# Order and PSUM banks of the last two down products in a nine-block attention + SwiGLU kernel

## The chip, the cores and the metric

The kernel runs on one NeuronCore of one Trainium2 chip. The metric is the device time of one execution in microseconds (us); the time before is the median of three executions. A profile is a separate, traced execution of the same kernel.

## What is computed

The reference, cut to what matters:

```python
# q, k, v: (8 batches, 8 heads, 576 positions, 64) ; g_norm: (64)
kv  = einsum('bhsd,bhse->bhde', k, v)
att = einsum('bhsd,bhde->bhse', q, kv)
x   = att / sqrt(mean(att * att, axis=-1) + 1e-6) * g_norm   # then laid out as (4608 tokens, 512)
g   = x @ w_gate                                             # 512 -> 1536
h   = g * (1 / (1 + exp(-g))) * (x @ w_val)                  # 512 -> 1536
out = h @ w_out                                              # 1536 -> 512, all float32
```

Only the last line, `out = h @ w_out` (called "down" in the code), is touched by the change, and only for the last 1024 of the 4608 tokens.

## The kernel before, in words

The 4608 tokens are cut into nine blocks of 512 (`BLK`), numbered 0 to 8 (`NB` = 9). For each block, attention makes `x`, the "up" step makes `h` (1536 features on partitions, 512 tokens), and the "down" step makes 512 rows of the output. Blocks 0 to 2 go one at a time (`alone`); blocks 3 to 8 go in pairs (3,4), (5,6), (7,8) (`Pair`). In a pair, up is done for both blocks together and then down for the first block (`pair.a.down`) and for the second (`pair.b.down`). After the pair (7,8) no block is left, so the last two downs are called with `nxt` = None and no attention work lies between their matmuls. The code's own loop order, together with `in_order` for TensorE, fixes the order of the matmuls there; the other engines run their instructions in the order in which the program issues them, each when its semaphores allow.

**Down as seven products.** `Down` (line 977, on top of `Quad`, line 640) multiplies a 2x2 arrangement of quarter matrices in the Winograd form of Strassen's method: seven products P1 to P7 instead of eight. Each product has 12 matmuls (two tiles e of 128 tokens, six steps over the features), each shown by the profile as 2 rows, so 24 rows. The results are put together like this, where o1 is the upper 256 tokens, o2 the lower 256, and left and right are the 256-column halves of the output:

```
S  = P1              o1 left  = S  + P2
U2 = P1 + P6         o1 right = U2 + P5 + P3
U3 = U2 + P7         o2 right = U3 + P5
                     o2 left  = U3 + P4
```

**Which bank a product goes to** is said by `CHAIN` (line 629). P1, P6, P7 and P4 are accumulated one onto another in one bank called b; P5 and P3 in a bank c; P2 has bank a. PSUM has eight banks here: b has 3 buffers, c has 2, a has 1, and a pool m has 2, which the last two downs leave unused. As U2 and U3 are partial sums inside bank b, ScalarE copies the bank out after P1 (`after1`, line 677), after P6 (`after6`, line 681), after P7 (`after7`, line 1043) and after P4 (`after4`, line 1047), and the next product of the chain can go into the bank only when the copy has read it.

For the very last block (`final`, block 8) the c bank is two banks, one for each tile e (`apart`), and P3 runs tile by tile (`order`, line 1011: all six steps of e = 0, then all six of e = 1), so that the first tile can be added and stored while the second is multiplied.

**What the operands wait for.** P7, P5 and P4 multiply sums of weight quarters that GpSimd makes (`turn_t`). P5 multiplies `s1`. P7 multiplies S3, which VectorE makes in place after P1 (`turn_s3`, line 1029), and P3 multiplies S4, which VectorE makes in place after P2, in `after2` (line 1037; in the profile these are rows of line 131, 128x1536, 1.75 us each). The S4 instruction comes after P2 because it overwrites P2's operand.

**The loop around it** is `Ffn.down` (line 1118). With `nxt` = None its order is 1, 5, 6, 7, 2, 4, 3. `after7` takes the ring buffer that o1 and o2 live in. The block's outputs are stored from `store` (line 1078) on SyncE's queue: o2 after P4 (512 KB), o1 after P3 (512 KB); in the last block o1 left after P2 (256 KB) and each tile of o1 right by itself (128 KB).

Of the kernel before, what the change touches and what calls it, by code (L numbers as in the profile page):

```python
# [8 lines left out]
F32 = mybir.dt.float32  # L9
# [5 lines left out]
P = 128  # L15
# [3 lines left out]
def kernel(  # L19
# [41 lines left out]
    nc = tc.nc  # L61

    B, H, S, D = q.shape
    NT, DM = out.shape
# [3 lines left out]
    HB = BLK // 2  # L68
    HD = DM // 2
# [10 lines left out]
    def pool(name, bufs, **kw):  # L80
        return ctx.enter_context(tc.tile_pool(name=name, bufs=bufs, **kw))
# [13 lines left out]
    m_psum = pool("m_psum", 2, space=PS)  # L95
# [34 lines left out]
    add = lambda e, o, a, b: e.tensor_tensor(out=o, in0=a, in1=b, op=OP.add)  # L130
# [21 lines left out]
    def ring():  # L152

        return r_pool.tile([P, 4, BLK], F32, name="r")

    class Words:
# [12 lines left out]
        def __init__(self, src, shape):  # L169
            self.raw = ld_pool.tile([P, LD], U32, name="ld")[:, 0 : 2 * BLK]  # L170
            dst = self.raw.rearrange("p (a b) -> p a b", a=shape[0])
            self.sent = nc.sync.dma_start(out=dst, in_=src)
            self.shape = shape
            self.begun = False
# [465 lines left out]
    class Quad:  # L640
# [11 lines left out]
        def multiply(self, p):  # L652
            name, first = CHAIN[p]
            if first:
                tiles = [PSUMS[name].tile([P, 2, HB], F32, name=name) for _ in range(1 + (name in self.apart))]
                self.ps[name], self.apart[name] = tiles[0], tiles[-1]
            banks = self.ps[name], self.apart[name]
            for e, i in self.order(p):
                lhsT, rhs = self.operands(p, e, i)

                self.ffn.multiplied = nc.tensor.matmul(  # L661
                    banks[e][:, e], lhsT=lhsT, rhs=rhs, start=first and i == 0 and (e == 0 or banks[0] is not banks[1]),
                    stop=i == self.steps - 1, skip_group_check=True,
                )
            getattr(self, f"after{p}", lambda: None)()

        def order(self, p):
            return [(e, i) for e in range(2) for i in range(self.steps)]
# [10 lines left out]
        def after6(self):  # L679
            self.u2 = self.piece(1)  # L680
            nc.scalar.copy(out=self.u2, in_=self.ps["b"])

    class Up(Quad):
# [22 lines left out]
        def after2(self):  # L706
            add(nc.vector, self.s, self.ps["a"], self.s)

        def after7(self):
            self.u3 = self.piece(2)  # L710
            copied = nc.scalar.copy(out=self.u3, in_=self.ps["b"])

            with tc.issue_after(copied.ins):
                nc.scalar.activation(out=self.s, in_=self.s, func=ACT.Silu)
            added = add(nc.vector, self.u3, self.ps["c"], self.u3)

            owed, self.ffn.owed = self.ffn.owed, None
            if owed:
                with tc.issue_after(added.ins):
                    owed()  # L720
# [232 lines left out]
    def chunks(t):  # L953

        return t.rearrange("p f (s c) -> p (f s) c", c=P) if len(t.shape) == 3 else t.rearrange("p a b c -> p (a b) c")

    def kept_steps(j, room):


        for i, (t, os) in enumerate(kept(j)):  # L960
            b11, b12, b22 = t[:, :, 0, 0], t[:, :, 0, 1], t[:, :, 1, 1]
            to = room[:, 8 * i : 8 * (i + 1)].rearrange("p (o r) c -> p o r c", r=4)
            t2_ = to[:, :, 0]
            yield lambda b22=b22, b12=b12, t2_=t2_: sub(nc.vector, t2_, b22, b12)
            yield lambda b11=b11, t2_=t2_: add(nc.vector, t2_, t2_, b11)
            yield lambda t=t, t2_=t2_, to=to: sub(
                nc.vector, to[:, :, 2:4], t[:, :, 1], t2_.unsqueeze(2).to_broadcast([P, 2, 2, P])
            )
            yield lambda t2_=t2_, os=os: send_leaf(j, os, (6,), t2_)
            yield lambda b11=b11, t2_=t2_, to=to: sub(nc.vector, to[:, :, 1], b11, t2_)  # L970
            yield lambda to=to, os=os: send_leaf(
                j, os, (7, 4, 5), to[:, :, 1:4].rearrange("p o r c -> p o (r c)")
            )
        if j < 2:
            yield from raw_steps(j)

    class Down(Quad):
        def __init__(self, ffn):
            super().__init__(NP)
            self.ffn = ffn  # L980
            self.t = {}
            self.final = ffn.n == NB - 1
            self.opens = None
            self.keeps = False
            if self.final:
                self.apart["c"] = None
# [13 lines left out]
                    )  # L1000
                self.t[p] += [t[:, 0], t[:, 1]]

        def multiply(self, p):
            super().multiply(p)
            if p in self.t and not self.keeps:
                stream.free(("T", p))
            if p == 7 and self.opens:
                stream.enable(self.opens)
            stream.pump()

        def order(self, p):
            order = [(e, i) for e in range(2) for i in range(self.steps)]
# [13 lines left out]
        def turn_s3(self):  # L1026

            pairs = self.ffn.h.rearrange("p (j e) t -> p e j t", e=2)
            sub(nc.vector, pairs[:, 0, :, 0:HB], pairs[:, 0, :, HB:BLK], pairs[:, 1, :, HB:BLK])

        def after2(self):
            add(nc.vector, self.o1[:, :, 0:HD], self.ps["a"], self.s)
            if self.final:
                self.ffn.store(self.o1[:, :, 0:HD], 0, slice(0, HD))

            pairs = self.ffn.h.rearrange("p (j e) t -> p e j t", e=2)
            self.s4 = sub(nc.vector, pairs[:, 1, :, 0:HB], pairs[:, 1, :, 0:HB], pairs[:, 0, :, HB:BLK])

        def after7(self):
            o = ring()  # L1040
            self.o1, self.o2 = o[:, 0:2], o[:, 2:4]
            u3 = self.piece(2)
            nc.scalar.copy(out=u3, in_=self.ps["b"])
            self.add_c(self.o2[:, :, HD:DM], u3)
# [21 lines left out]
    class Ffn:  # L1066
# [51 lines left out]
        def down(self, nxt, then={}):  # L1118

            down = self.down_  # L1120
            fill = nxt.steps() if nxt else {}
            for p in (1, 6, 5, 7, 2, 4, 3) if 5 in fill else (1, 5, 6, 7, 2, 4, 3):
                if p == 1 and 7 not in down.t:
                    down.turn_t(7, self.ended)
                if p == 6 and 4 not in down.t:
                    down.turn_t(4, nxt.halves[0] if nxt and nxt.n >= TURNED else None)

                with tc.issue_after(nxt.multiplied.ins) if self.n == 0 and p in (5, 6) else ExitStack():
                    down.multiply(p)
                self.make(12)  # L1130
                if p in fill:
                    fill[p]()
                if p in then:
                    then[p]()
                if p in (5, 7) and self.n == 1:

                    with tc.issue_after(nxt.scaled.ins), tc.issue_after(nxt.placed.ins):
                        for step in kept_steps(2 + (p == 7), chunks(ring() if p == 7 else xi_alone)):
                            step()
                if p == 1:  # L1140

                    with tc.issue_after(nxt.q_turned.ins) if self.n == 0 else ExitStack():
                        down.turn_s3()

        def plain_up(self, f, halves=(0, 1)):

            if 0 in halves:
                self.ps[f] = [pool.tile([P, 2, HB], F32, name=pool.name[0]) for pool in (b_psum, c_psum)]
            of = slice(halves[0], halves[-1] + 1)
            ps = [t[:, of] for t in self.ps[f]]  # L1150
            x = self.att.x[:, 0:4].rearrange("p (h m) i t -> p (m i) h t", h=2)
            for t, w in zip(ps, (wg, wv)):
                for i in range(NS):
                    nc.tensor.matmul(
                        t, lhsT=w[f // 2][:, i, P * (f % 2) : P * (f % 2 + 1)], rhs=x[:, i, of],
                        start=(i == 0), stop=(i == NS - 1),
                    )
            h = self.h[:, f].rearrange("p (h t) -> p h t", h=2)[:, of]
            nc.scalar.activation(out=h, in_=ps[0], func=ACT.Silu)
            mul(nc.vector, h, h, ps[1])  # L1160
# [208 lines left out]
    for n in range(PAIRED, NB, 2):  # L1369
        pair = Pair(n)  # L1370
        after = blocks[n + 2 : n + 5]
        fill = {}
        if after:
# [9 lines left out]
            fill = {5: first_kv, 11: second_kv}  # L1383
# [45 lines left out]
```

## Time and profile before

| | |
|---|---|
| median of three executions | 1023.85 us (1022.38 to 1024.58) |
| the profiled execution: its own time | 1026.13 us |
| the profiled execution: span of the profile | 1024.4 us |
| TensorE busy | 998.7 us, 97% of the span |
| VectorE / ScalarE / GpSimd busy | 667.3 / 232.1 / 369.8 us |
| mean granted TensorE clock | 0.997 |
| down of block 7, first matmul to the first of block 8 | 946.42 to 983.65 us |
| down of block 8, first matmul to the end of the last | 983.65 to 1021.01 us |

How to read the profile: times are counted from the start of the span. PE is TensorE's matmuls, PEld its weight loads, DVE is VectorE, ACT ScalarE, POOL GpSimd, SPq SyncE's queue, from which the stores are issued. A row of a timeline has the start, the length, the engine, the line of the kernel, the operation and "output<-input" by the names of the tiles; consecutive rows of a kind are merged with their number (x24), and what stands in brackets is how long the engine had been idle before and what the profile takes for the releaser. Matmuls overlap: a row of 24 lasts 5.34 us, but the next product can start 5.18 us after it.

### The profile page before, as it was taken

The numbers are of one execution on the slowest core, as the hardware profiler recorded it, in microseconds if no ns is written. First come the engines' busy times: TensorE is split into PE (matmuls) and PEld (weight loads), VectorE is DVE, ScalarE is ACT, GpSimd is POOL, SyncE is SP. The second block draws the span as 40 slices with busy tenths as digits, with TensorE's granted clock in tenths as the row PEclk, the third lists the DMA queues.
The fourth block names the chain that finished last, engine by engine and source line by source line (L and its number), as shares of the span: only waits on it lengthen the run. The fifth ranks groups of instructions, "written<-read, shape, count | busy, mean of one in ns | idle before, by whom it ended". The sixth has DMA issues, their size and how long they took to land.

```text
span 1024.4 us, 17093 instructions
## 1 busy us (share of the span) xinstructions
PE 998.7 (97%) x6506; PEld 832.7 (81%) x6506; DVE 667.3 (65%) x1118; ACT 232.1 (23%) x367; POOL 369.8 (36%) x290
## 2 busy tenths in 40 slices
PE   5999999999999799999999999999999999999998
PEld 4544688888888688888888888888888888888887
DVE  2998897759767475666666846666767566666211
ACT  2765111221122212121111212112112121121100
POOL 0000363525444140454556003554650026546600
PEclk9999999999999899999999999999999999999999
DMA  7689643656566925676753265667321655553011
GB/s 218 200 266 251 118 88 134 217 165 147 165 140 113 227 58 162 167 208 164 169 144 51 89 159 152 160 173 179 101 34 50 144 160 146 150 145 95 1 42 42
DMA packets 254290, 143.23 MB, mean 140 GB/s; under 512 B 149504, under 2 KB 236544, under 8 KB 254208
## 3 DMA queue, kind: packets, MB, share of 16 engines
q1 hardware_dynamic: 223488, 138.20, 50.2%
q10 hardware_dynamic: 30656, 3.94, 2.4%
q8 instruction: 52, 0.85, 0.4%
q14 instruction: 30, 0.25, 0.1%
q0 software_dynamic: 64, 0.00, 0.0%
HBM read 104.99 MB, written 28.70 MB: 131 GB/s over the span
## 4 chain that ended last, share of the span: by engine, by line
PE 76%; DVE 9%; DMA 5%; SPq 5%; issue 2%; ACT 2%; POOL 1%; DVEq 0%; POOLq 0%; ACTq 0%
PE b L811 21%; PE b L661 21%; PE c L661 11%; PE c L811 10%; PE a L661 5%; PE a L811 5%; SPq L333 2%; DVE r L190 1%; PE m L431 1%; DMA ld<-in_moe_w_out_dram 1%; DVE arena L131 1%; PE m L370 1%; DVE arena L199 1%; SPq L522 1%; DMA ld<-in_v_dram 1%
## 5 line engine op out<-in xcount | busy, mean ns | idle before, releaser
L811 PE MATMUL b<-arena,t 128*128 128x256 f32 x1008 | 244.6, 381 | 0.0
L811 PEld LDWEIGHTS b<-arena,t 128*128 128x128 f32 x1008 | 189.9, 190 | 29.9 <-DVE r L130 2.8
L130 POOL TENSOR_TENSOR r<-r 128x256 f32<-128x256 f32 (+1 forms) x90 | 94.8, 1054 | 246.2 <-DMA t<-w 149.5
L130 DVE TENSOR_TENSOR r<-b,r 128x512 f32<-128x512 f32 (+1 forms) x234 | 139.0, 607 | 61.1 <-PE b L811 56.0
L130 DVE TENSOR_TENSOR r<-c,r 128x512 f32<-128x512 f32 (+1 forms) x170 | 104.7, 624 | 108.6 <-PE c L811 41.1
L131 POOL TENSOR_TENSOR t<-wo 128x512 f32<-128x512 f32 x54 | 78.1, 1468 | 175.9 <-DVE wo L130 107.2
L132 POOL TENSOR_TENSOR arena<-r 128x1024 f32<-128x1024 f32 (+1 forms) x54 | 100.9, 1883 | 112.3 <-DVE r L130 84.4
L130 DVE TENSOR_TENSOR r<-a,r 128x512 f32<-128x512 f32 x93 | 59.2, 637 | 110.5 <-PE a L661 73.6
L811 PE MATMUL c<-arena,t 128*128 128x256 f32 x504 | 122.5, 379 | 1.0 <-ACT r L825 0.8
L131 DVE TENSOR_TENSOR arena<-arena 128x512 f32<-128x512 f32 (+3 forms) x96 | 104.3, 1102 | 18.1 <-PE b L661 14.0
L811 PEld LDWEIGHTS c<-arena,t 128*128 128x128 f32 x504 | 95.6, 190 | 14.7 <-ACT r L825 1.2
L661 PE MATMUL b<-wo,arena 128*128 128x256 f32 x432 | 98.3, 382 | 0.4 <-issue 0.3
L661 PE MATMUL b<-t,arena 128*128 128x256 f32 x432 | 96.4, 379 | 1.4 <-POOL s L130 0.7
L661 PEld LDWEIGHTS b<-t,arena 128*128 128x128 f32 x432 | 81.9, 190 | 13.2 <-POOL s L130 1.1
L661 PEld LDWEIGHTS b<-wo,arena 128*128 128x128 f32 x432 | 81.2, 190 | 12.7 <-DVE arena L132 0.9
L825 ACT COPY r<-b 128x512 f32<-128x512 f32 x54 | 31.6, 585 | 191.2 <-PE b L811 191.2
L131 POOL TENSOR_TENSOR t<-arena 128x512 f32<-128x512 f32 x36 | 51.4, 1438 | 59.5 <-DMA w<-t 23.3
L811 PE MATMUL a<-arena,t 128*128 128x256 f32 x252 | 66.1, 379 | 0.0
L811 PEld LDWEIGHTS a<-arena,t 128*128 128x128 f32 x252 | 47.9, 190 | 6.5
L661 PE MATMUL c<-wo,arena 128*128 128x256 f32 x216 | 48.2, 379 | 0.2 <-DVE r L130 0.2
L661 PE MATMUL c<-t,s 128*128 128x256 f32 x216 | 48.1, 379 | 0.0
L661 PE MATMUL a<-wo,arena 128*128 128x256 f32 x216 | 48.1, 379 | 0.0
(105 smaller groups left out, 1228.5 us busy)
## 6 DMA issues: line engine op xcount, KB each, us to landing
t<-w SPq DMA_DIRECT2D x180, 256.0 KB, 3.1
out_dram<-r SPq DMA_DIRECT2D x17, 512.0 KB, 2.9
ld<-in_k_dram SPq DMA_DIRECT2D x26, 288.0 KB, 4.8
ld<-in_v_dram SPq DMA_DIRECT2D x26, 288.0 KB, 5.9
t<-w SPq DMA_DIRECT2D x54, 128.0 KB, 2.4
ld<-in_moe_w_gate_dram SPq DMA_DIRECT2D x12, 512.0 KB, 4.7
ld<-in_moe_w_val_dram SPq DMA_DIRECT2D x12, 512.0 KB, 4.6
ld<-in_moe_w_out_dram SPq DMA_DIRECT2D x12, 512.0 KB, 5.5
```

Of the source, the lines that this page charges most:

```text
L130: add = lambda e, o, a, b: e.tensor_tensor(out=o, in0=a, in1=b, op=OP.add)
L131: sub = lambda e, o, a, b: e.tensor_tensor(out=o, in0=a, in1=b, op=OP.subtract)
L132: mul = lambda e, o, a, b: e.tensor_tensor(out=o, in0=a, in1=b, op=OP.mult)
L190: return nc.vector.scalar_tensor_tensor(out=mag, in0=mag, scalar=3, in1=sign, op0=OP.logical_shift_left, op1=OP.bitwise_xor)
L199: return nc.vector.tensor_tensor(out=dst.bitcast(U32), in0=self.mag.rearrange("p (a b) -> p a b", a=a, b=b), in1=unit.bitcast(U32).rearran ...
L333: queue.dma_start(out=to[32 * r : 32 * (r + 1), j, g0:g1], in_=q[b, 4 * i + 2 * j + h, s0 : s0 + 32 * (g1 - g0), 32 * d : 32 * (d + 1)].re ...
L370: self.positions = nc.tensor.matmul(self.kv_ps[r][u * D : (u + 1) * D, g, :], lhsT=k[:, u, c, :], rhs=v[:, u, c, :], start=(c == 0), stop= ...
L431: self.multiplied = nc.tensor.matmul(self.ps[i][u][p : p + D, t, j, :], lhsT=self.qt[rows, tile_t, head, p : p + D], rhs=kvs[b % 3][rows, ...
L522: placed = queue.dma_start(out=dst[rows[b], :, rows[a]], in_=src[rows[a], :, rows[b]])
L661: self.ffn.multiplied = nc.tensor.matmul(banks[e][:, e], lhsT=lhsT, rhs=rhs, start=first and i == 0 and (e == 0 or banks[0] is not banks[1 ...
L811: self.ffn.multiplied = nc.tensor.matmul(ps[:, i], lhsT=stream.use(self.ffn.n, self.j, o, p), rhs=self.operand(o, p), start=first and i == ...
L825: nc.scalar.copy(out=dst, in_=ps)
```

## The change

In the last two downs (`lone`: `nxt` is None) four things are different:

- The order of the products is P1, P5, P6, P2, P7, P3, P4. In block 8, P3 is cut: its tile e = 0 runs after P7, then P4, and then its tile e = 1 as the last matmuls of the kernel.
- P3 is no longer accumulated onto P5 in bank c. It goes to banks of pool m (`third`): one for block 7, two for block 8.
- As P3's bank no longer holds P5, VectorE adds P5 to U2 ahead of time, straight after ScalarE's copy of U2 (`after6` calls `add_c(self.u2, self.u2)`). The end of P3 is then m + (U2 + P5).
- The ring buffer of o1 and o2 is taken in `after2` and not in `after7`.

All products, matmuls and stores remain the same in number and size; block 7 has one VectorE addition more (128x512), block 8 two (128x256).

```diff
@@ class Down
+            self.lone = False
...
-        def multiply(self, p):
+        def multiply(self, p, es=(0, 1)):
+            if p == 3 and self.lone:
+                self.third(es)
+                return
             super().multiply(p)
...
+        def third(self, es):
+            if es[0] == 0:
+                tiles = [m_psum.tile([P, 2, HB], F32, name="m") for _ in range(1 + self.final)]
+                self.thirds = tiles[0], tiles[-1]
+            for e in es:
+                for i in range(self.steps):
+                    lhsT, rhs = self.operands(3, e, i)
+                    self.ffn.multiplied = nc.tensor.matmul(
+                        self.thirds[e][:, e], lhsT=lhsT, rhs=rhs, start=i == 0 and (e == 0 or self.final),
+                        stop=i == self.steps - 1, skip_group_check=True,
+                    )
+            if not self.final:
+                add(nc.vector, self.o1[:, :, HD:DM], self.thirds[0], self.u2)
+                self.ffn.store(self.o1, 0)
+                return
+            for e in es:
+                add(nc.vector, self.o1[:, e, HD:DM], self.thirds[e][:, e], self.u2[:, e])
+                self.ffn.store(self.o1[:, e : e + 1, HD:DM], e, slice(HD, DM))
+
+        def after6(self):
+            super().after6()
+            if self.lone:
+                self.add_c(self.u2, self.u2)
...
+        def rows(self):
+            o = ring()
+            self.o1, self.o2 = o[:, 0:2], o[:, 2:4]
+
         def after2(self):
+            if self.lone:
+                self.rows()
             add(nc.vector, self.o1[:, :, 0:HD], self.ps["a"], self.s)
...
         def after7(self):
-            o = ring()
-            self.o1, self.o2 = o[:, 0:2], o[:, 2:4]
+            if not self.lone:
+                self.rows()
             u3 = self.piece(2)
@@ Ffn.down
-            for p in (1, 6, 5, 7, 2, 4, 3) if 5 in fill else (1, 5, 6, 7, 2, 4, 3):
+            down.lone = nxt is None
+            order = (1, 6, 5, 7, 2, 4, 3) if 5 in fill else (1, 5, 6, 7, 2, 4, 3)
+            if down.lone:
+                order = (1, 5, 6, 2, 7, 3, 4)
+            for p in order:
...
-                    down.multiply(p)
+                    down.multiply(p, *[(0,)] * (p == 3 and down.lone and down.final))
...
+            if down.lone and down.final:
+                down.multiply(3, (1,))
```

## The prediction, made before the changed kernel was run

> **What bounds the kernel now.** I read the busy shares first: TensorE is busy for 97% of the span, so only its idle time, and what lies after its last matmul, can be saved.
>
> ```profile
> PE 998.7 (97%) x6506; PEld 832.7 (81%) x6506; DVE 667.3 (65%) x1118; ACT 232.1 (23%) x367; POOL 369.8 (36%) x290
> ```
>
> The change touches only the last two downs, so I next read TensorE's timeline from 945 us on, one row for each product.
>
> ```profile
> 956.78 5.34 PE L661 MATMUL b<-wo,arena 128*128 128x256 f32 x24
> 962.85 5.42 PE L661 MATMUL b<-t,arena 128*128 128x256 f32 x24 [0.72 <-POOL s L130]
> 968.11 5.34 PE L661 MATMUL a<-wo,arena 128*128 128x256 f32 x24
> 973.29 5.34 PE L661 MATMUL b<-t,arena 128*128 128x256 f32 x24
> ...
> 994.01 5.34 PE L661 MATMUL b<-wo,arena 128*128 128x256 f32 x24
> 1000.02 5.45 PE L661 MATMUL b<-t,arena 128*128 128x256 f32 x24 [0.68 <-ACT r L681]
> 1005.31 5.34 PE L661 MATMUL a<-wo,arena 128*128 128x256 f32 x24
> 1010.49 5.34 PE L661 MATMUL b<-t,arena 128*128 128x256 f32 x24
> 1015.67 5.34 PE L661 MATMUL c<-wo,arena 128*128 128x256 f32 x24
> ```
>
> In each block the rows are P6, P7, P2, P4 and (shown for block 8) P3. Undisturbed, product follows product at 5.18 us (968.11 to 973.29, 1005.31 to 1010.49, 1010.49 to 1015.67). Brackets stand at P7 only, once in each block: these are the only two pauses of TensorE in both downs. What P7 waits for is in ScalarE's timeline and in the table of waits:
>
> ```profile
> 962.16 0.59 ACT L681 COPY r<-b 128x512 f32<-128x512 f32 x1 [9.77 <-PE b L661]
> 999.39 0.58 ACT L681 COPY r<-b 128x512 f32<-128x512 f32 x1 [9.77 <-PE b L661]
> ```
> ```profile
> PE b L661 <- POOL s L130: 0.7, 1, 0.7
> PE b L661 <- ACT r L681: 0.7, 1, 0.7
> ```
>
> The copies of U2 end at 962.75 and 999.97; P7 starts at 962.85 and 1000.02, 0.05 to 0.1 us later. The profile names GpSimd for block 7. I take that for the copy as well: the bracket in block 8 is the same within 0.04 us although GpSimd does nothing there, and the GpSimd instruction that it can mean ended at 962.23, half a microsecond too early. So both pauses are one mechanism: P6 and P7 are neighbours in one accumulating bank, and U2 has to be read out between them.
>
> Last, the tail: SyncE's issues and the DMA in quarters of a microsecond, where the last two columns are the share of the DMA engines and GB/s.
>
> ```profile
> 1015.87 0.58 ACT L1047 COPY r<-b 128x512 f32<-128x512 f32 x1 [9.78 <-PE b L661]
> 1021.05 0.42 DVE L130 TENSOR_TENSOR r<-c,r 128x256 f32<-128x256 f32 x1 [2.17 <-PE c L661]
> 1021.50 0.34 SPq L1078 DMA_DIRECT2D out_dram<-r  x1
> ```
> ```profile
> 1017.00:1017.25 0.25, 0.25 (x3) 0.23 (x2) 0.00 (x0) 0.00 (x0) 0.00 (x0) 1.00 0.00 0
> 1017.25:1017.50 0.25, 0.25 (x3) 0.22 (x2) 0.00 (x0) 0.00 (x0) 0.00 (x0) 1.00 0.47 180
> ...
> 1018.75:1019.00 0.25, 0.25 (x3) 0.22 (x2) 0.14 (x1) 0.00 (x0) 0.00 (x0) 1.00 0.06 17
> ...
> 1022.25:1022.50 0.25, 0.00 (x0) 0.00 (x0) 0.00 (x0) 0.00 (x0) 0.00 (x0) 1.00 0.53 184
> ```
>
> The copy of o2 left ends at 1016.46, and its 512 KB store moves data from about 1017.4 to 1018.8, so from 0.9 to 2.3 us after. The last matmul ends at 1021.01; addition, issue at 1021.50, 128 KB that move from about 1022.4 and land 1.7 us after issue, and 1.2 us of closing make the 1024.4.
>
> **What the Trainium skill says.** "PSUM — Partial Sum Buffer", section on bank collisions: accesses of two engines to one bank must be kept apart by semaphores, by bank and not by address. The trace agrees: P7 starts only after the copy of its own bank (0.05 to 0.1 us), while the copy after P7 (L1043, 968.31) runs beside P2 in bank a with no bracket. "Perfetto Trace Analysis", section Optimizing Tensor Performance: independent groups should rotate through banks, so that the evacuation of one is covered by the next group's matmuls. That is what the copies after P1, P7 and P4 show, and the one after P6 doesn't. "DMA: Bandwidth & Descriptors", anatomy of one DMA: the cost is mostly fixed, about 2 us, plus bytes over the rate; the page's fit is for the software path, and here the trace has the durations, 1.7 us for 128 KB and 2.8 us for 512 KB, which I use.
>
> **The change part by part.** The sum is made on the profiled execution, whose span is 1024.4 us and whose own time is 1026.13 us, 2.3 us above the median of the runs, 1023.85. I carry the difference, not the level, over to the median.
>
> *P2 between P6 and P7.* From the start of P6 to the start of P2 there are two products: 11.33 us in block 7 (956.78 to 968.11) and 11.30 us in block 8 (994.01 to 1005.31). Undisturbed it would be 2 x 5.18 = 10.36. The pauses cost 0.97 + 0.94 = 1.91 us; this is more than the brackets, 1.40, as pipelining across the joint and the pace of the first rows behind it are lost too. With P2 in between, the copy, which ends 0.8 us after the moment at which P6's successor can start (961.96, copy 962.75), has 5.18 us of cover. P2 needs nothing new: bank a is empty, its weights and its operand are raw. If P7 still waited for anything, GpSimd among it, that would now come 5.18 us after P6's end; the sums of the next block that GpSimd works on end at 967.25, and P7 waits only for their predecessors, the weight sums. Gain 1.91 us.
>
> *P3 after P7, before P4.* P4 follows P7 in bank b and needs the copy of U3 (the same 0.8 us); P2 was its cover, now it is P3, 5.18 us in block 7 and half of it, 2.59 us, in block 8. No cost. P3 waits for S4. After P2, VectorE adds o1 left (0.69 us, from 973.49) and makes S4 (1.75 us, from 974.10), so S4 is there at 975.85, 2.55 us after P2's successor has started (973.29). P4 was the cover, P7 is it now, again 5.18 us, so 2.6 us are to spare. Zero; without this cover it would be 2.55 us in each block.
>
> *P3 in banks of pool m.* The pool's earlier users are parts of the attention, long over. Block 8 reuses block 7's bank only after the addition at the end of block 7's P3. The matmuls have the same shape; I see no reason for another pace, as b, c and a have the same 5.34 us. Zero. It also takes P3 free of bank c, so that o2 right (which reads P5 there) is in no one's way.
>
> *U2 + P5.* One VectorE row more in block 7 at 0.69 us (as the row of o2 right, 128x512) and two in block 8 at 0.42 us. VectorE is idle for most of P6 to P2 (its bracket before o2 right is over 15 us). Queued behind it are o1 left and S4, 5 us later. Zero on the path.
>
> *The ring buffer taken at P2.* It is one of five, and its last readers are the up step's rows around 950 us. Zero; not below, as nothing waited for it.
>
> *Stores.* Block 7's o1 store is issued earlier and o2's later; nothing waits for either. In block 8 P4 now ends 2.59 us before the last matmul and not 5.18, so o2's 512 KB are issued later against the end. By the clock after the change: TensorE ends at 1021.01 - 1.91 = 1019.10, P4 at 1016.51, the copy at about 1017.15. The data move 0.9 to 2.3 us after, that is from 1018.05 to 1019.45. The last store is issued at 1021.50 - 1.91 = 1019.59, and its data begin 0.8 us later, at about 1020.4. The two are 0.9 us apart, and o2 lands at 1017.15 + 2.8 = 1019.95, before the last one at 1021.3. Zero is taken; bounds: nothing, up to 1.1 us if the last store took 2.8 instead of 1.7 us. A gain is excluded, since the last tile's chain of addition and store is the same.
>
> Sum: 1024.4 - 1.91 = 1022.5 us of span, and 1023.85 - 1.91 = 1021.94 for the median, 0.19% less.
>
> **The rivals.**
> (a) *The tail gives part of it back*: the last 128 KB queue up behind the 512 KB. For it: the gap shrinks from 3.6 us (1018.8 to 1022.4) to 0.9, and stores in this kernel took up to 4.9 us to land. Against it: that was with other transfers on the queues, and here none is left. Up to 1.1 us are lost, 1023.0.
> (b) *One pause stays*, because the named GpSimd sum really holds P7 of block 7. Against it: the times above. It would be 1023.85 - 0.94 = 1022.9.
> (c) *Slower: P3 stalls on S4.* VectorE's chain behind P2 must fit into P7. It decides from 5.18 us on; measured are 2.55. To end more than 0.2% above the time before, it would have to add 1.91 + 2.05 = 3.96 us over two blocks, so last 7.2 us in each. VectorE has nothing else queued there, apart from the addition of U2 + P5, which is done 3 us or more before. This would give 1026 or more.
> (d) *The brackets are the true price*, 1.40 us: 1022.45. It is part of the forecast's range.
>
> **How the numbers follow.** About 0.2% (2.05 us) is what a measurement of this kernel can tell from no change; the bound lies at 1021.80, just below the forecast. Chances: forecast with (d) 0.82, (a) 0.09, (b) 0.05, (c) 0.02, and 0.02 for a larger gain of unknown cause. The three runs before lie up to 1.5 us off their median, so the forecast's case falls on the two sides of 1021.80 nearly evenly, slightly more above: 0.40 faster, 0.42 same, with a trace of slower. (a) and (b) end within 0.2%. In all faster 0.42, same 0.55, slower 0.03. The range takes about a microsecond of scatter about 1021.9 on either side and reaches to (a) and (b) with some: 1020.7 to 1023.3.
>
> **What would show it.** TensorE's timeline from 945 us on without brackets, 5.18 us from product to product, and its last matmul ending 1.9 us earlier; the copies of line 681's kind beside rows of bank a; S4 ended 2.6 us before P3 starts; the last store landing 1.7 us after its issue. The prediction is wrong if a bracket appears at P7, P3 or P4, or if the last store takes longer than 1.7 us.

## The result and the profile after

| | before | after |
|---|---|---|
| median of 17 executions each | 1023.71 us | 1021.87 us |
| lowest to highest | 1021.90 to 1026.28 | 1020.25 to 1024.07 |
| ratio after to before, 95% interval | | 0.9982 (0.9974 to 0.9991) |
| the profiled execution: its own time / its span | 1026.13 / 1024.4 us | 1022.13 / 1020.4 us |
| first matmul of block 7's down (start) | 946.42 us | 944.32 us |
| from there to the end of the span ("the stretch") | 77.94 us | 76.03 us |
| last matmul's end to the end of the span ("the tail") | 3.35 us | 3.35 us |

The median fell by 1.84 us; 1.91 were forecast. The kernel is faster, since the interval lies below 1, but by 0.18%, just inside the 0.2% that the prediction took for the least that can be told.

The two spans differ by 4.0 us, more than twice the gain. 2.10 of these are there before the change begins: block 7's down starts at 944.32 and not at 946.42, although the two programs are the same up to there. Only the stretch belongs to the change: 77.94 - 76.03 = 1.91 us. All experiments below are therefore read on the stretch, each from one profiled execution. It is a steady measure: the changed kernel and two kernels of the experiments that have no pause either agree in it within 0.01 us (76.03 and twice 76.04).

TensorE's timeline of the changed kernel, from block 7's P6 on (start, length, engine, line, operation, tiles):

```profile
954.68 5.34 PE L661 MATMUL b<-wo,arena 128*128 128x256 f32 x24
959.86 5.34 PE L661 MATMUL a<-wo,arena 128*128 128x256 f32 x24
965.04 5.34 PE L661 MATMUL b<-t,arena 128*128 128x256 f32 x24
970.22 5.34 PE L1024 MATMUL m<-wo,arena 128*128 128x256 f32 x24
975.40 5.34 PE L661 MATMUL b<-t,arena 128*128 128x256 f32 x24
...
1006.48 2.75 PE L1024 MATMUL m<-wo,arena 128*128 128x256 f32 x12
1009.07 5.34 PE L661 MATMUL b<-t,arena 128*128 128x256 f32 x24
1014.25 2.75 PE L1024 MATMUL m<-wo,arena 128*128 128x256 f32 x12
```

These are P6, P2, P7, P3, P4, and at the end block 8's half of P3, P4, and the other half. There are no brackets any more, and every start is 5.18 us after the one before (2.59 for a half P3). The table of TensorE's waits is empty from block 7's first product on. On ScalarE the copies stand where they stood, right after their product; only what runs beside them is another bank's work:

```profile
960.06 0.58 ACT L681 COPY r<-b 128x512 f32<-128x512 f32 x1 [9.78 <-PE b L661]
...
996.32 0.58 ACT L681 COPY r<-b 128x512 f32<-128x512 f32 x1 [9.78 <-PE b L661]
...
1014.45 0.59 ACT L1083 COPY r<-b 128x512 f32<-128x512 f32 x1 [7.18 <-PE b L661]
```

VectorE around P2, P7 and P3 of block 7: the new addition of P5 to U2, o1 left, S4, o2 right, and o1 right.

```profile
960.68 0.69 DVE L130 TENSOR_TENSOR r<-c,r 128x512 f32<-128x512 f32 x1 [9.01 <-ACT r L681]
965.24 0.69 DVE L130 TENSOR_TENSOR r<-a,r 128x512 f32<-128x512 f32 x1 [3.87 <-PE a L661]
965.85 1.75 DVE L131 TENSOR_TENSOR arena<-arena 128x1536 f32<-128x1536 f32 x1
971.04 0.69 DVE L130 TENSOR_TENSOR r<-c,r 128x512 f32<-128x512 f32 x1 [3.44 <-ACT r L1079]
975.61 0.69 DVE L130 TENSOR_TENSOR r<-m,r 128x512 f32<-128x512 f32 x1 [3.87 <-PE m L1024]
```

The new row is done at 961.37, almost 4 us before VectorE is wanted again. S4 is there at 967.60; P3 starts at 970.22, 2.6 us later.

The tail, in quarters of a microsecond (share of the DMA engines and GB/s in the last two columns):

```profile
1015.75:1016.00 0.25, 0.25 (x3) 0.21 (x2) 0.00 (x0) 0.00 (x0) 0.00 (x0) 1.00 0.15 57
...
1017.25:1017.50 0.25, 0.00 (x0) 0.00 (x0) 0.22 (x1) 0.00 (x0) 0.00 (x0) 1.00 0.29 99
...
1018.25:1018.50 0.25, 0.00 (x0) 0.00 (x0) 0.00 (x0) 0.00 (x0) 0.00 (x0) 1.00 0.55 193
```

o2's 512 KB move from about 1016.0 to 1017.3, the last 128 KB from 1018.3 on. Between them nothing moves for almost a microsecond, so the last store isn't held up.

### The profile page after: what moved, and what is told of

It is laid out like the page before. It is cut to its first block, busy times and chain, and to the rows that moved or that the text cites. A ratio compares the mean times of both kernels' runs of the same rounds, so it can differ in the third digit from the quotient of the medians.

```text
span 1020.4 us, 17100 instructions
## 1 busy us (share of the span) xinstructions
PE 998.4 (98%) x6506; PEld 833.3 (82%) x6506; DVE 667.2 (65%) x1121; ACT 232.4 (23%) x367; POOL 368.4 (36%) x290
## 4 chain that ended last, share of the span: by engine, by line
PE 80%; DVE 9%; SPq 4%; DMA 4%; ACT 2%; issue 1%; POOL 0%; DVEq 0%; ACTq 0%; POOLq 0%
PE b L661 22%; PE b L811 22%; PE c L661 11%; PE c L811 11%; PE a L661 5%; PE a L811 5%; SPq L333 2%; PE m L431 1%; DVE r L190 1%; PE m L370 1%; DVE arena L131 1%; DVE arena L199 1%; DMA ld<-in_moe_w_out_dram 1%; PE m L1024 1%; SPq L522 1%
## 5 line engine op out<-in xcount | busy, mean ns | idle before, releaser
L811 PE MATMUL b<-arena,t 128*128 128x256 f32 x1008 | 244.6, 381 | 0.0
L130 POOL TENSOR_TENSOR r<-r 128x256 f32<-128x256 f32 (+1 forms) x90 | 94.7, 1054 | 246.3 <-DMA t<-w 149.6
L130 DVE TENSOR_TENSOR r<-b,r 128x512 f32<-128x512 f32 (+1 forms) x234 | 138.9, 607 | 61.2 <-PE b L811 56.1
L130 DVE TENSOR_TENSOR r<-c,r 128x512 f32<-128x512 f32 (+1 forms) x170 | 104.6, 624 | 87.2 <-PE c L811 40.5
L130 DVE TENSOR_TENSOR r<-a,r 128x512 f32<-128x512 f32 x93 | 59.2, 637 | 110.9 <-PE a L661 73.8
L661 PE MATMUL b<-arena,t 128*128 128x256 f32 x192 | 46.8, 387 | 0.0
```

The lines of the kernel that those rows point to most:

```text
L661: self.ffn.multiplied = nc.tensor.matmul(banks[e][:, e], lhsT=lhsT, rhs=rhs, start=first and i == 0 and (e == 0 or banks[0] is not banks[1 ...
L811: self.ffn.multiplied = nc.tensor.matmul(ps[:, i], lhsT=stream.use(self.ffn.n, self.j, o, p), rhs=self.operand(o, p), start=first and i == ...
```

## The experiments

The theory: in each of the last two blocks TensorE paused at P7, because P7 goes into bank b behind P6 and the copy of U2 has to read b in between; the change puts P2 there, and P3 in a bank of its own keeps the next joint of the chain covered. A joint is the place where one product of the chain P1, P6, P7, P4 follows another in bank b; it is covered when TensorE has work in another bank while the copy reads b. Against the theory stood that GpSimd holds P7 of block 7, that the tail or the order alone makes the gain, and that other waits are near to taking its place. "Cost" below is what a pause adds to the stretch: the time from the start of the product before it to the start of the product after the paused one, less what that takes without a pause (2 x 5.18 us, or 5.18 + 2.59 where the paused one is half a P3).

### Each block alone

Two kernels, each with one of the two new lines (the remarks behind # are only here):

```diff
-            down.lone = nxt is None
+            down.lone = nxt is None and not down.final     # block 7 only
+            down.lone = nxt is None and down.final         # block 8 only
```

> The change in block 7 alone; block 8 keeps the old order and banks. Read on the stretch from the first matmul of block 7's down to the end of the span: 77.94 us before, 76.05 after. Theory (each block's pause is the wait of P7 for the copy of U2, and the two are separate): no bracket in block 7, the bracket of 0.7 us at P7 of block 8 stays, stretch 77.94 - 0.96 = 76.98. Rival (GpSimd holds P7 of block 7, so that the gain comes from block 8 or from the tail): stretch stays near 77.9.

> The change in block 8 alone, with its cut P3. Same stretch. Theory: the bracket of 0.7 us at P7 of block 7 stays, none in block 8, stretch 77.94 - 0.94 = 77.00. Rival (the cut P3 changes the tail as well): stretch other than 77.0, with another length from the last matmul to the end than the 3.35 us of both kernels.

Measured: the stretch is 76.98 us with block 7 alone and 76.99 with block 8 alone, and the tail is 3.35 both times. Each kernel keeps the bracket of the block that was left as it was; here are their tables of TensorE's waits, block 7 alone changed and then block 8 alone changed:

```profile
PE b L661 <- ACT r L681: 0.7, 1, 0.7
```
```profile
PE b L661 <- POOL s L130: 0.7, 1, 0.7
```

It follows that the two gains are separate and add up, 0.96 + 0.95 = 1.91, and that the cut P3 neither adds to the tail nor takes from it.

### The copy itself, and GpSimd's name

The kernel before, in its old order, without the copy of U2 in the last two blocks, so that S stands in U2's place:

```diff
+        def after6(self):
+            if self.ffn.n < NB - 2:
+                super().after6()
+                return
+            self.u2 = self.s
```

> The kernel before with its own order and banks, without the copy of U2 in the last two blocks: S stands in its place in the output of o1 right, so one ScalarE copy and the sum with P6 there are left out. P7 follows P6 in bank b with nothing reading in between. Theory (the copy is all that P7 waits for, in block 7 too): no bracket at P7 in either block, P7 starts 5.18 us after P6, stretch 76.05 with the old order. Rival (GpSimd holds P7 of block 7): the bracket of 0.7 us in block 7 stays, stretch 77.0.

Measured: a stretch of 76.04 us, with no bracket. P6 and P7 of block 7, and the GpSimd row that the bracket had named, in the kernel before and here:

```profile
956.45 5.34 PE L661 MATMUL b<-wo,arena 128*128 128x256 f32 x24
961.63 5.34 PE L661 MATMUL b<-t,arena 128*128 128x256 f32 x24
```
```profile
959.75 2.48 POOL L130 TENSOR_TENSOR s<-arena 128x512 f32<-128x512 f32 x2
...
959.43 2.48 POOL L130 TENSOR_TENSOR s<-arena 128x512 f32<-128x512 f32 x2
```

GpSimd's two instructions start 2.98 us after P6's start, as in the kernel before (2.97), and P7 starts at 961.63 while the second of them runs until 961.91. So P7 doesn't need them. The name "POOL s L130" in the bracket of block 7 was wrong: the whole wait was the copy's.

### P2 ahead of P7, the rest as before

As o1 is written after P2, the ring buffer is taken at P2 here too; the cut leaves these lines out.

```diff
...
-            for p in (1, 6, 5, 7, 2, 4, 3) if 5 in fill else (1, 5, 6, 7, 2, 4, 3):
+            for p in (1, 6, 5, 7, 2, 4, 3) if 5 in fill else (1, 5, 6, 2, 7, 4, 3):
```

> The kernel before, with P2 and P7 exchanged in the last two blocks and nothing else: P1, P5, P6, P2, P7, P4, P3, with P3 onto P5 in bank c as before (the ring buffer is taken at P2). Theory (every product of bank b needs another bank's product ahead of it): the pause moves from P7 to P4, which now follows P7 in bank b and waits for the copy of U3; a bracket of about 0.7 us at P4 in both blocks, stretch as before, 77.9. Rival (the pause belongs to P7, or to its operands): no bracket, stretch 76.05.

Measured: a stretch of 77.98 us. P7 has no bracket now, P4 has it, in both blocks, as TensorE's timeline shows (P7 and P4 of block 7, then of block 8):

```profile
964.48 5.34 PE L661 MATMUL b<-t,arena 128*128 128x256 f32 x24
970.59 5.42 PE L661 MATMUL b<-t,arena 128*128 128x256 f32 x24 [0.77 <-ACT r L1049]
...
1001.74 5.34 PE L661 MATMUL b<-t,arena 128*128 128x256 f32 x24
1007.76 5.45 PE L661 MATMUL b<-t,arena 128*128 128x256 f32 x24 [0.68 <-ACT r L1049]
```

It follows that the wait moves with the neighbourhood in bank b. There are three joints in the chain P1, P6, P7, P4, and P5, P2 and P3 are the three products that can lie between. So where whole products are to be the cover, P3 has to go in front of P4. Whether it also needs a bank other than c is what the next run tries.

### P3 in front of P4, but still in bank c

```diff
-                tiles = [m_psum.tile([P, 2, HB], F32, name="m") for _ in range(1 + self.final)]
-                self.thirds = tiles[0], tiles[-1]
+                self.thirds = self.ps["c"], self.apart["c"]
...
-                        self.thirds[e][:, e], lhsT=lhsT, rhs=rhs, start=i == 0 and (e == 0 or self.final),
+                        self.thirds[e][:, e], lhsT=lhsT, rhs=rhs, start=False,
...
             super().after6()
-            if self.lone:
-                self.add_c(self.u2, self.u2)
```

> The changed order with the cut P3, but P3 goes onto P5 in bank c as before, without banks of its own and without adding P5 to U2 beforehand. As o2 right = U3 + P5 has to be read from bank c before P3 goes into it, P3 waits for the copy of U3 and then for VectorE's addition. Theory (the banks of its own are needed to make P3 a cover): a bracket at P3 of about 1.4 us in block 7 (0.6 for the copy, 0.7 for the addition) and 1.0 to 1.4 in block 8, each costing some 0.2 us more by the joint: stretch 76.05 + 1.6 + 1.4 = 79.0, slower than before (77.94). Rival (the order alone brings the gain): stretch 76.05.

Measured: a stretch of 79.11 us, 1.17 longer than before the change. P3 waits for the copy of U3 (in block 7 it ends at 972.78) and behind it for o2 right's addition (973.51):

```profile
973.56 5.45 PE L1023 MATMUL c<-wo,arena 128*128 128x256 f32 x24 [1.40 <-DVE r L130]
...
1011.23 2.86 PE L1023 MATMUL c<-wo,arena 128*128 128x256 f32 x12 [1.14 <-DVE r L130]
```

The pauses cost 1.67 and 1.40 us. It follows that the new order without the banks of its own would have been a loss; order and banks are one change and not two.

### The cut of block 8's P3

```diff
-                    down.multiply(p, *[(0,)] * (p == 3 and down.lone and down.final))
+                    down.multiply(p)
...
-            if down.lone and down.final:
-                down.multiply(3, (1,))
```

> The changed kernel with block 8's P3 left whole after P7, so that P4 is last and the 512 KB store of o2 ends the kernel. Theory: TensorE's last matmul ends as in the changed kernel, but the tail has the copy of 128x512 (0.59 us, against 0.42 for the last addition) and a store that lands in 2.8 us and not in 1.7: about 1.25 us longer than 3.35, stretch 76.05 + 1.25 = 77.3, so most of one block's gain is lost. Rival (the tail is a fixed cost, whatever is stored last): stretch 76.05 to 76.2.

Measured: a stretch of 77.27 us; TensorE has no bracket and the tail is 4.59 us. The median is 1023.17 us against 1023.55 in the same series, ratio 0.9997 (0.9988 to 1.0005): two thirds of the gain are gone and no difference can be told. The tail, and the table of DMA issues of that kernel from 1012 us on (last column: us from issue to landing):

```profile
1016.94 0.59 ACT L1083 COPY r<-b 128x512 f32<-128x512 f32 x1 [9.77 <-PE b L661]
1017.55 0.38 SPq L1114 DMA_DIRECT2D out_dram<-r  x1
```
```profile
out_dram<-r SPq DMA_DIRECT2D x1, 512.0 KB, 2.8
out_dram<-r SPq DMA_DIRECT2D x1, 128.0 KB, 1.7
```

A copy of 0.59 in place of an addition of 0.42, and 2.8 us of landing in place of 1.7, make up the 1.24 us within the rounding. So where P3 goes ahead of P4 for the sake of the pauses, P4 with its larger store must not come last; the change keeps half of P3 for the end.

### How near the next wait is

S4 is made by three instructions in place of one, so that it is late:

```diff
-            self.s4 = sub(nc.vector, pairs[:, 1, :, 0:HB], pairs[:, 1, :, 0:HB], pairs[:, 0, :, HB:BLK])
+            for f in (sub, add, sub) if self.lone else (sub,):
+                self.s4 = f(nc.vector, pairs[:, 1, :, 0:HB], pairs[:, 1, :, 0:HB], pairs[:, 0, :, HB:BLK])
```

> The changed kernel with S4 made by three VectorE instructions in a row in place of one (subtract, add the same, subtract; 1.75 us each), so that it is ready 2 x 1.75 = 3.5 us later. In the changed kernel S4 is ready 2.6 us before P3 could start. Theory (P3 depends on S4 only, with this margin): 0.9 us of wait at P3 in each block, with the joint's 0.2 about 1.1 each, stretch 76.05 + 2.2 = 78.2. Rival (P3 has more slack, or its wait is hidden by the weight loads): stretch 76.05. Rival (the slack is smaller than I read): more than 78.5.

Measured: a stretch of 78.28 us; the bracket at P3 is 0.85 us in each block and costs 1.12.

```profile
971.44 5.45 PE L1024 MATMUL m<-wo,arena 128*128 128x256 f32 x24 [0.85 <-DVE arena L131]
```

The third instruction ends at 971.39, P3 starts 0.05 us later. So P3 hangs on S4 and on nothing slower, and the 2.6 us of slack are real: counted from P7's start, S4 came 3.58 us later than in the changed kernel (6.14 and 2.56 us), and P3 started 1.01 us later (6.19 and 5.18 us).

### Another cure: the chain's bank by tiles

The kernel before with its order of products, but with bank b as two banks, one for each tile, P6, P7 and P4 tile by tile, and each copy in two.

```diff
+            self.cut = ffn.n >= NB - 2
+            if self.cut:
+                self.apart["b"] = None
...
+        def copy_b(self, to):
+            if not self.cut:
+                return nc.scalar.copy(out=to, in_=self.ps["b"])
+            for e, b in enumerate((self.ps["b"], self.apart["b"])):
+                nc.scalar.copy(out=to[:, e], in_=b[:, e])
...
-            return order if p == 3 and self.final else sorted(order, key=lambda ei: ei[1])
+            return order if p == 3 and self.final or self.cut and p in (6, 7, 4) else sorted(order, key=lambda ei: ei[1])
...
```

> The kernel before with its own order of products and without any use of pool m; instead the chain's bank b is two banks in the last two blocks, one for each tile e, P6, P7 and P4 run tile by tile, and each copy is two of 128x256. While P6's second tile is multiplied (2.59 us), the first tile's U2 can be read, and while P7's first tile is multiplied, the second's. Theory (all that is missing at P6 to P7 is some other bank's work between a copy and its successor, about 0.9 us of it): no bracket in either block, stretch 76.05 as for the change, with the tail of 3.35 us. Rival (a product has to come between, since the two copies are too slow or serialize): a bracket of 0.2 to 0.7 us at P7, stretch 76.5 to 77.9. Rival (the cut of bank b costs something else, at P1 of block 8, which takes over block 7's banks): a bracket there.

Measured: a stretch of 76.04 us, with no bracket, and a median of 1022.05 against 1023.75 us in the same series, ratio 0.9985 (0.9977 to 0.9994). The copies of U2 of block 7, one while P6's second tile runs, one while P7's first does (P7 starts at 961.82):

```profile
959.43 0.37 ACT L995 COPY r<-b 128x256 f32<-128x256 f32 x1 [7.40 <-PE b L661]
962.02 0.37 ACT L995 COPY r<-b 128x256 f32<-128x256 f32 x1 [2.22 <-PE b L661]
```

It is as fast as the change, with the old order of products and without the addition of P5 to U2. Neither cure leaves a pause in the stretch, so neither has more to win there from the waits: what is left is 14 products at 5.18 us and the tail.

## Why the prediction was right

*The pauses.* Both went, and the sum of 1.91 us, counted from product to product and not from the brackets, is what the stretch lost. Rival (d), the brackets' 1.40 us as the full price, is out: block 7 alone gave 0.96, block 8 alone 0.95.

*Whose wait it was.* The prediction put block 7's bracket down to the copy against the profile's word. Leaving the copy out showed it right, and rival (b) out.

*P3 before P4, in banks of its own.* Forecast at nothing, measured at nothing. The prediction named the copy of U3 as what P3 covers in front of P4, but of the banks of its own it said only that they keep o2 right out of everyone's way, without a price. The run in bank c shows what that is worth: 3.07 us over both blocks (79.11 for 76.04), more than the whole gain. The step was right and its weight was not seen.

*S4.* The slack was forecast at 2.6 us and measured at 2.6. Rival (c), the one on the slower side, needs a chain 2.6 us longer before it begins, and the run with a late S4 cost 1.12 us in each block once it was overrun. The price that the prediction gave for P3 without P7 as its cover, 2.55 us, was not tried.

*The tail.* Forecast: 0.9 us between the two stores' data, and no loss. Measured: from about 1017.3 to 1018.3, and a tail of 3.35 us in both kernels. Rival (a) is out for this size of store. The cut of P3, which the prediction took for granted, is what keeps the tail so: without it 1.24 of the 1.91 us are lost.

*The median.* It came to 1021.87 us for 1021.94 and on the side of "within 0.2%", which had the larger chance by little (0.55 to 0.42). That the two agree to 0.07 us is partly luck: the three runs that the forecast started from had a median 0.14 us above that of all 17 (1023.85 and 1023.71), and the gain came out 0.07 us short. The medians alone would not have ruled out rivals (b) and (d) either, since their interval allows a gain from 0.9 to 2.7 us; the stretch rules them out. What was left out is how much profiles differ ahead of the change: over the profiles of all ten kernels block 7's down starts between 943.01 and 946.42 us, and most of that is there after the first 143 us (by then 140.67 to 143.09 us for the same matmul). Where in the start-up it comes from wasn't tried.

## What to carry to other kernels

Where partial sums are read out in the middle of an accumulating chain, every joint of the chain needs at least as much work of another bank as the read-out lasts (here a read-out ended 0.8 us after the next product could have started; the smallest cover tried was 2.59 us, so how little would do is not shown). Count the joints and the products that can lie between them, or cut the chain's bank by tiles so that one tile covers the other. Price a pause from start to start of the work around it and not by the idle time shown, check the releaser that a profile names by its end time, and compare two profiles only over the part that the change touches. When work is reordered near the end of a kernel, look at which store comes last: here the tail was 3.35 us with 128 KB last and 4.59 us with 512 KB.

## What the runs showed that was not expected

A pause of TensorE cost a nearly constant amount more than its bracket. The matmul rows here last 0.379 us and start every 0.216 us. In seven of the ten pauses in these profiles the cost was the bracket and 0.27 us: 0.68 cost 0.94 (before, block 8), 0.85 cost 1.12, 1.14 cost 1.40 and 1.40 cost 1.67. 0.16 of it is the overlap of a row with the next (0.379 - 0.216), which is lost at a pause, and 0.10 is the first row after it, whose successor starts 0.320 us later and not 0.216.

In the other three it was the bracket and 0.24 us: 0.72 cost 0.96 (before, block 7, and again with block 8 alone changed) and 0.77 cost 1.00, to the nearest hundredth (P4 of block 7 with P2 ahead of P7). There the first weight load started 0.03 us ahead of its matmul row, and the row's successor came after 0.291 us. All three are P7 or P4 of block 7, which multiply weight sums that GpSimd has made in the same down; whether that is the reason was not tried.
